# Fifteen extra small loads on ScalarE's DMA queue at the start of a decode kernel

## The chip, the cores and the metric

The kernel runs on one core of one Trainium2 chip. A core has a matrix engine (TensorE, PE in the profile), a vector engine (VectorE, DVE), a scalar engine (ScalarE, ACT), GpSimd (POOL) and SyncE (SP), which here issues the large loads. Sixteen DMA engines move data between HBM and the on-chip memory (SBUF, 128 partitions). The metric is the device time of one execution in microseconds, lower is better: before the change, a median of 381.85 us over three runs (381.73 to 382.11).

## What is computed

One token of a decoder goes through two branches, mixed by a gate:

```python
g = _sigmoid((x * gate_w).sum(-1, keepdims=True))
a = _A_ref(x, A_k_cache, A_v_cache, A_wq, A_wo)
b = _B_ref(x, B_w_in, B_w_sp, B_b_sp, B_w_out)
return g * a + (1 - g) * b
```

Branch A is grouped-query attention for one query position: `x` (1024 values) times `A_wq` (1024 x 4096) gives 32 query heads of 128. They share 4 key/value heads with 65536 cached positions each: scores against `A_k_cache`, softmax, weighted sum of `A_v_cache`, and a product with `A_wo` (4096 x 1024). Branch B is a small gated MLP with one position: `x @ B_w_in` (1024 x 3584), GELU, a layer norm of one half, scaling by `B_w_sp` and a shift by `B_b_sp` (one number each), a product with the other half, and `B_w_out` (1792 x 1024). All tensors are bf16. The two caches are 67 MB each; with the weights some 162 MB are read once.

## The kernel before

**Recording and emission.** The kernel calls `P(engine, function, r=..., w=..., dma=...)` for each operation. A `Recorder` notes which keys an operation reads and writes, works out the waits, and `emit` (from L96) writes each engine's instructions in the recorded order, with semaphore waits in front. A DMA adds 16 to a semaphore of its own name when it has landed. The engines run in order, so a waiting instruction holds up everything behind it on its engine. Two numbers, `R.ahead = 2` and `R.early = 4`, say how many of the first DMAs of SyncE and of ScalarE are moved ahead of the start barrier. At the end SyncE waits for the stores of the output (L122).

**Memory.** One SBUF tensor, the `arena`, holds all regions; a list of names and sizes (from L193) lays them out one behind the other. The first, `RING`, is the landing area of the large loads.

**The large loads.** `load` appends them to a list, and `issue` (L376 to L392) issues the next one on SyncE as soon as the piece of the ring that it overwrites has been used up. The order is A_wq, k(0) with k(1), B_w_in, k(2), k(3), B_w_out, then the remaining keys and values in turn, and A_wo last, whose last quarter is cut into 1280, 512 and 256 KB. Each load has 128 rows, one for each partition, of up to 64 KB. All are issued at L389.

**The small loads.** ScalarE issues four (L288): `x` and `gate_w` as 8 rows of 256 bytes, and the single numbers `B_w_sp` and `B_b_sp`, one row of 2 bytes each. All four stand ahead of the start barrier.

**The start.** `x` is spread over the partitions (L427, L432, L436). At L437 TensorE copies `B_w_sp` and `B_b_sp` to all partitions. DVE forms the gate's products (L442, L443), TensorE sums them (L444), ScalarE takes the exponential (L446, behind the load of its function table), and DVE finishes the gate (L447 to L451). TensorE then multiplies `x` by A_wq (recorded at L260 and L262, as all large matmuls are), and DVE casts and places the queries (L467, L474, L482).

**The body.** For each piece of 16384 positions `k_piece` transposes the keys on DVE in four steps (L502) and multiplies them on TensorE; `score_pair` (L519) takes scores out of PSUM, `exp_pair` (L534) exponentiates on ScalarE, `pt_pair` (L539) transposes, and `pv_piece` multiplies by the values. `mixer_piece`, `mixer_rest` and `wout_piece` do branch B between the first key pieces. The next load into a slot of the ring is issued when its last user, a transpose or a matmul, is done.

**The end.** `wo_rows` and `wo_piece` (L712) multiply by A_wo as its pieces land, DVE casts the result (L775), and SyncE stores 2 KB (L366).

Of the kernel before, what the change touches and what calls it, by code (L numbers as in the profile page):

```python
# [17 lines left out]
class Recorder:  # L18
# [77 lines left out]
    def emit(self, nc):  # L96
        waits = self.plan()
        sems = {e: nc.alloc_semaphore("eng_" + e) for e in self.ENGINES}
        dsem = {k: nc.alloc_semaphore("dma_%s" % k) for k in self.dma_count}
        final = {k: v for k, v in self.dma_count.items()}  # L100

        def run(eng, handle):
            for o, ws in zip(self.ops, waits):
                if o.eng != eng:
                    continue
                for d in ws:
                    if d.dma:
                        handle.wait_ge(dsem[d.dma[0]], d.dma[1])
                    else:
                        handle.wait_ge(sems[d.eng], d.count)  # L110
                last = o.fn(handle)
                if o.dma:
                    last.then_inc(dsem[o.dma[0]], 16)
                elif o.inc:
                    last.then_inc(sems[eng], 1)

        body = nc.cur_bb.bb
        gate = next(i for i, x in enumerate(body.instructions)
                    if isinstance(x, mybir.InstDrain) and x.engine == mybir.EngineType.SP)
        first = len(body.instructions)  # L120
        run("SP", nc.sync)
        nc.sync.wait_ge(dsem["out"], final["out"])  # L122
        made = list(body.instructions)
        moved = made[first:first + self.ahead]
        assert all(isinstance(x, mybir.InstDMACopy) for x in moved)
        body.instructions = made[:gate] + moved + made[gate:first] + made[first + self.ahead:]
        run("POOL", nc.gpsimd)
        run("PE", nc.tensor)
        first = len(body.instructions)
        run("ACT", nc.scalar)  # L130
        made = list(body.instructions)
        gate = next(i for i, x in enumerate(made) if isinstance(x, mybir.InstDrain) and x.engine == mybir.EngineType.Activation)
        moved = made[first:first + self.early]
        assert all(isinstance(x, mybir.InstDMACopy) for x in moved)
        body.instructions = made[:gate] + moved + made[gate:first] + made[first + self.early:]
        run("DVE", nc.vector)


def bass_gated_mix__gqa_block_cached__mixer_gmlp__decode_kernel(
# [23 lines left out]
    FC = FH // 128  # L163
# [12 lines left out]
    QW = DO // NW  # L176
# [11 lines left out]
    def region(name, nbf):  # L188
        nonlocal cur
        OFF[name] = cur  # L190
        cur += (nbf + 15) // 16 * 16

    for name, n in [  # L193
        ("RING", NSUB * SUB), ("KT", NKT * 4096), ("SC", NSC * 2048), ("PSB", 2 * 1024), ("PTSB", 2 * 1024),
        ("QPAD", 4 * QP), ("IDB", 128), ("BM", 256), ("SEL", 16 * 32),
        ("M16", 32), ("MQ", 32), ("XT", KC), ("WB", 2), ("WBB", 4), ("ONEB", 128),
        ("MAXC", 2 * total), ("LP", 2 * total), ("COLS", 2 * 64), ("DM", 64), ("ONES", 256), ("QALL", 128), ("OVZ", 32 * OC + 31), ("E4Z", 128), ("MHALF", 4),
        ("YB", FC), ("OROW", QW),
    ]:
        region(name, n)  # L200
    NA = (cur + 63) // 64 * 64
# [2 lines left out]
    def ab(name, n, o=0):  # L204
        return arena[:, OFF[name] + o:OFF[name] + o + n]
# [4 lines left out]
    def vw(base, off, dims, p0=0, np_=128):  # L210
        ps = base.ap[0][0]
        return bass.AP(tensor=base.tensor, offset=base.offset + off + p0 * ps,
                       ap=[[ps, np_]] + [list(d) for d in dims])
# [41 lines left out]
    P = R.op  # L255
# [42 lines left out]
    small(wb[0:1, 1:2], B_b_sp.rearrange("(a n) -> a n", a=1), "bsp")  # L298

    stream = []
    place = {}
# [41 lines left out]
    for i in range(6):  # L345
        a = 2 * i + 4
# [83 lines left out]
    def f(e):  # L430
        for c in range(KC):
            ins = e.matmul(tb[:, c:c + 1], vw(xm, c, [[8, 128]], 0, 8), oneb[0:8, 0:1], start=(c == 0),  # L432
                           stop=(c == KC - 1), skip_group_check=True)
        return ins
# [374 lines left out]
```

## Time and profile before

| What | Value |
|---|---|
| Median of three runs | 381.85 us (381.73 to 382.11) |
| Span of the profiled execution | 380.3 us |
| The profiled execution's own total time | not given beside its span |
| Mean granted TensorE clock | 0.838 of full speed |
| Bytes read | 162.01 MB, 426 GB/s over the span |
| Busy | TensorE 62%, DVE 54%, ScalarE 6%, GpSimd 2% of the span |

The span runs from the first to the last instruction of the profiled execution. DMA queues have numbers: q1 carries SyncE's DMAs, q10 ScalarE's, q8 instructions fetched while the program runs. A DMA is cut into packets that the sixteen engines work off, and the share of a queue is the time of its packets as a part of sixteen engines' span. In a narrow window a packet counts whole where it starts. An instruction marked ACTq or SPq is the issuing of a DMA, not its transfer. In the timeline each line has the start, the duration, the engine, the line of the kernel and the operands, and in brackets the idle time before it with what ended it. The chain of waits is followed back from the last instruction.

### The profile page before, as it was taken

The numbers are of one execution on the slowest core, as the hardware profiler recorded it, in microseconds if no ns is written. First come the engines' busy times: TensorE is split into PE (matmuls) and PEld (weight loads), VectorE is DVE, ScalarE is ACT, GpSimd is POOL, SyncE is SP. The second block draws the span as 40 slices with busy tenths as digits, with TensorE's granted clock in tenths as the row PEclk, the third lists the DMA queues.
The fourth block names the chain that finished last, engine by engine and source line by source line (L and its number), as shares of the span: only waits on it lengthen the run. The fifth ranks groups of instructions, "written<-read, shape, count | busy, mean of one in ns | idle before, by whom it ended". The sixth has DMA issues, their size and how long they took to land.

```text
span 380.3 us, 2581 instructions
## 1 busy us (share of the span) xinstructions
PE 235.1 (62%) x1449; PEld 58.1 (15%) x836; DVE 204.6 (54%) x162; ACT 23.3 (6%) x24; POOL 8.4 (2%) x37
## 2 busy tenths in 40 slices
PE   0061388458558924895788138952895884739378
PEld 0010011011111200122112001220121110212015
DVE  4011496778389525965892249745774882312020
ACT  1000000010420000002200000022000000220000
POOL 5000000000000000000000000000000000000000
PEclk9998599696859985998699859995899697958689
DMA  9999999999999999999999999999999999999996
GB/s 435 427 420 400 469 388 438 441 469 431 401 414 441 441 443 427 434 410 424 477 441 434 434 434 414 415 441 441 434 407 433 445 441 441 436 403 424 419 426 262
DMA packets 4254, 162.17 MB, mean 426 GB/s; under 512 B 532, under 2 KB 532, under 8 KB 788
## 3 DMA queue, kind: packets, MB, share of 16 engines
q1 hardware_dynamic: 4208, 162.01, 98.9%
q8 instruction: 9, 0.15, 0.2%
q10 hardware_dynamic: 36, 0.00, 0.0%
q14 instruction: 1, 0.01, 0.0%
HBM read 162.01 MB, written 0.00 MB: 426 GB/s over the span
## 4 chain that ended last, share of the span: by engine, by line
DMA 56%; PE 23%; DVE 18%; ACT 1%; issue 1%; SPq 0%; ACTq 0%; DVEq 0%
DMA arena<-in_A_k_cache_dram 34%; DVE arena L502 15%; DMA arena<-in_A_wo_dram 10%; DMA arena<-in_A_v_cache_dram 8%; PE scp L260 7%; PE scp L262 6%; DMA arena<-in_B_b_sp_dram 5%; PE obt L260 4%; PE obt L262 4%; DVE arena L539 1%; PE fbt L712 1%; PE fbt L660 1%; ACT arena L534 1%; SPq L389 0%; ACTq L288 0%
## 5 line engine op out<-in xcount | busy, mean ns | idle before, releaser
L502 DVE STREAM_TRANSPOSE arena<-arena 128x2048 f32<-128x2048 f32 x64 | 143.0, 2284 | 48.2 <-DMA arena<-in_A_k_cache_dram 32.7
L260 PE MATMUL scp<-arena 128*128 128x512 bf16 (+1 forms) x275 | 112.8, 429 | 87.7 <-DVE arena L502 86.3
L262 PE MATMUL scp<-arena 128*128 128x512 bf16 (+1 forms) x279 | 113.1, 427 | 0.0
L260 PE MATMUL obt<-arena 128*64 128x512 bf16 (+2 forms) x334 | 62.9, 419 | 17.5 <-DMA arena<-in_A_v_cache_dram 17.5
L262 PE MATMUL obt<-arena 128*64 128x512 bf16 (+2 forms) x334 | 62.2, 414 | 0.0
L260 PEld LDWEIGHTS scp<-arena 128*128 128x128 bf16 (+1 forms) x275 | 27.7, 104 | 200.1 <-issue 101.3
L539 DVE STREAM_TRANSPOSE arena<-arena 128x2048 bf16<-128x2048 bf16 x7 | 16.2, 2311 | 28.5 <-PE obt L262 26.4
L534 ACT ACTIVATE arena<-arena 128x2048 bf16<-128x2048 f32 x8 | 16.0, 2002 | 218.6 <-DVE arena L531 195.6
L260 PEld LDWEIGHTS obt<-arena 128*64 128x64 bf16 (+1 forms) x334 | 18.3, 113 | 70.7 <-issue 56.1
L519 DVE TENSOR_SCALAR_CACHE_REDUCE arena<-scp 128x2048 f32<-128x2048 f32 x8 | 18.3, 2292 | 16.0 <-PE scp L262 16.0
L580 PE MATMUL mbt<-arena 128*128 128x128 bf16 x16 | 1.9, 258 | 12.6 <-DVE arena L575 12.6
L542 DVE STREAM_TRANSPOSE arena<-arena 128x1024 bf16<-128x1024 bf16 x2 | 2.5, 1246 | 12.7 <-PE obt L262 12.7
L490 POOL COPY arena<-arena 32x32 bf16<-32x32 bf16 x16 | 3.2, 203 | 234.5 <-PE scp L262 209.7
L568 DVE RECIPROCAL arena<-mbt 128x1 f32<-128x1 f32 x4 | 0.6, 139 | 14.1 <-PE mbt L563 14.1
L531 DVE TENSOR_REDUCE arena<-mbt 128x1 f32<-128x32 f32 x4 | 0.8, 192 | 13.5 <-PE mbt L528 13.5
L437 PE MATMUL mbt<-arena 1*128 1x2 bf16 x1 | 0.2, 158 | 12.3 <-DMA arena<-in_B_b_sp_dram 12.3
L439 DVE COPY arena<-mbt 128x2 f32<-128x2 f32 x1 | 0.2, 160 | 12.3 <-PE mbt L437 12.3
L775 DVE CAST arena<-fbt 36x128 bf16<-36x128 f32 x1 | 0.3, 283 | 11.0 <-PE fbt L712 11.0
L432 PE MATMUL scp<-arena 8*128 8x1 bf16 x8 | 0.7, 199 | 8.7 <-DVE arena L427 8.7
L712 PE MATMUL fbt<-arena 128*32 128x128 bf16 x128 | 4.1, 220 | 0.1
L712 PEld LDWEIGHTS fbt<-arena 128*32 128x32 bf16 x128 | 3.6, 97 | 1.6 <-DMA arena<-in_A_wo_dram 0.8
L467 DVE CAST arena<-obt 97x1024 bf16<-97x1024 f32 x1 | 1.2, 1225 | 4.9 <-PE obt L262 4.9
(91 smaller groups left out, 54.2 us busy)
## 6 DMA issues: line engine op xcount, KB each, us to landing
arena<-in_A_k_cache_dram SPq DMA_DIRECT2D x6, 4096.0 KB, 33.1
arena<-in_A_v_cache_dram SPq DMA_DIRECT2D x2, 4096.0 KB, 26.0
arena<-in_B_w_in_dram SPq DMA_DIRECT2D x1, 7168.0 KB, 30.4
arena<-in_A_wo_dram SPq DMA_DIRECT2D x3, 2048.0 KB, 33.4
arena<-in_B_w_out_dram SPq DMA_DIRECT2D x1, 3584.0 KB, 21.5
arena<-in_A_wo_dram SPq DMA_DIRECT2D x1, 1280.0 KB, 30.3
arena<-in_A_wo_dram SPq DMA_DIRECT2D x1, 512.0 KB, 31.0
arena<-in_A_wo_dram SPq DMA_DIRECT2D x1, 256.0 KB, 30.8
```

The source lines that it names most:

```text
L260: return e.matmul(*a, **kw)
L262: one = e.matmul(*a, **kw).ins
L467: P("DVE", lambda e: e.tensor_copy(psb[0:97, :], ob[0:97, :]), w=["psb", "ob"])
L490: P("POOL", lambda e, pb=pb: e.tensor_copy(vw(qpad, 24 + 32 * pb, [[QP, 4], [1, 8]], 32 * pb, 32), vw(qall, 8 * g, [[32, 4], [1, 8]], 32 * ...
L502: P("DVE", lambda e: e.transpose(ktb(i).bitcast(F32), sl[:, 4096 * p:4096 * (p + 1)].bitcast(F32)), r=keys[4 * p:4 * p + 4], w=[("kt", i % ...
L519: P("DVE", lambda e: e.tensor_scalar(scs(j), scp[:, :], 0.0, None, op0=ALU.add, op1=ALU.max, accum_out=maxc[:, j:j + 1]), w=[("sc", j % 2) ...
L534: P("ACT", lambda e: e.activation(psb2, scs(j), ACTF.Exp, bias=gcol(j // 2, K_NB), scale=SCALE, accum_out=lp[:, j:j + 1]), r=[("sc", j % 2 ...
L539: P("DVE", lambda e: e.transpose(ptsb2, psb2), r=["psb"], w=[("ptsb", 0), ("ptsb", 1)])
L542: P("DVE", lambda e: e.transpose(ptsb(n), ab("PSB", 1024, 1024 * (n % 2))), r=["psb"], w=[("ptsb", n % 2)])
L580: ins = e.matmul(mb[:, 0:128], sel[:, 128 * c:128 * (c + 1)], osc[:, 128 * c:128 * (c + 1)], start=(c == 0), stop=(c == 3))
L660: ins = e.matmul(fb[32 * b:32 * (b + 1), 0:QW], e4z[0:97, 31 - j:63 - j], part[0:97, QW * s:QW * (s + 1)], start=(first and s % (NW // 2) ...
L712: ins = e.matmul(fb[32 * b:32 * (b + 1), 0:QW], ovz[:, z:z + 32], sl[:, o:o + QW], start=False, stop=(i == 3 and c == 7), tile_position=(0 ...
```

## The change

A strip `TINY` of 128 bf16 elements per partition is added behind all other regions of the arena. Behind its four small loads ScalarE issues fifteen more: load k (1 to 15) takes k rows of 8 elements (16 bytes) from the first k rows of A_wq, 8192 bytes apart, and writes them to partitions 0 to k-1 of the strip, at columns of its own. Nothing reads the strip. `R.early` stays at 4, so the fifteen stand behind the start barrier and ahead of ScalarE's first table load. All count on one semaphore, `tiny`, and SyncE waits for its full count at the end, behind the wait for the output. The order of all other instructions on every engine is the same as before.

```diff
         nc.sync.wait_ge(dsem["out"], final["out"])
+        nc.sync.wait_ge(dsem["tiny"], final["tiny"])
         made = list(body.instructions)
...
-        ("YB", FC), ("OROW", QW),
+        ("YB", FC), ("OROW", QW), ("TINY", 16 * 8),
     ]:
...
     small(wb[0:1, 1:2], B_b_sp.rearrange("(a n) -> a n", a=1), "bsp")
 
+    for k in range(1, 16):
+        def f(e, k=k):
+            with nc.allow_non_contiguous_dma(reason="a few bytes"):
+                return e.dma_start(ab("TINY", 8, 8 * k)[0:k, :], A_wq[0:k, 8 * k:8 * k + 8])
+        P("ACT", f, w=[("tiny", k)], dma="tiny")
```

## The prediction

> **What bounds the kernel now.** I read the page's totals first, then the windows of ten microseconds, then the chain of waits near the end, then the DMA queues in narrow windows, and last ScalarE's and SyncE's own timelines. The page says:
>
> ```profile
> span 380.3 us, 2581 instructions
> PE 235.1 (62%) x1449; PEld 58.1 (15%) x836; DVE 204.6 (54%) x162; ACT 23.3 (6%) x24; POOL 8.4 (2%) x37
> DMA  9999999999999999999999999999999999999996
> q1 hardware_dynamic: 4208, 162.01, 98.9%
> q8 instruction: 9, 0.15, 0.2%
> q10 hardware_dynamic: 36, 0.00, 0.0%
> ```
>
> No compute engine is busy for more than 62% of the span, while the sixteen DMA engines are busy in every slice but the last. Queue q1 (SyncE's loads) alone takes 98.9% of their time. So the kernel is bound by its loads, and something costs time only if it makes a DMA engine busy longer, leaves the load queue empty, or lengthens the stretch after the last landing. That stretch is in the chain of waits:
>
> ```profile
> 331.05 37.33 DMA arena<-in_A_wo_dram
> ...
> 376.50 1.77 PE fbt L712 x56
> 378.27 0.01 issue
> 378.27 0.42 PE fbt L712 x8
> ...
> 378.79 0.28 DVE arena L775
> ```
>
> and, for what the last eight matmuls wait for, in the timeline of the same stretch:
>
> ```profile
> 378.27 0.23 PEld L712 LDWEIGHTS fbt<-arena 128*32 128x32 bf16 x8 [0.18 <-DMA arena<-in_A_wo_dram]
> ```
>
> The last 256 KB of A_wo release the last eight matmuls at 378.27. Issued at 347.44 and 30.8 us on the way, they land at 378.24. A load counts as landed when the slowest of its DMA engines is done, so the span is the slowest engine's finishing time plus 380.3 - 378.27 = 2.03 us.
>
> The profiled execution's span is 380.3 us. Its own total is not among the figures shown, so I make the sum against the span and carry the difference to the median of the three timed runs, 381.85 us; the 1.55 us between them is taken as fixed. Those three runs spread over 0.38 us (381.73 to 382.11). I call 0.2% (0.76 us) about what a measurement can tell from no change.
>
> **The change, part by part.** Nothing is removed. Four things are added.
>
> *1. Fifteen issues on ScalarE.* They stand behind the start barrier, ahead of the table load for the gate's exponential (L446). ScalarE now does this:
>
> ```profile
> 0.72 0.28 ACTq L288 DMA_DIRECT2D arena<-in_gate_w_dram  x1
> 1.03 0.27 ACTq L288 DMA_DIRECT2D arena<-in_B_w_sp_dram  x1
> 1.34 0.27 ACTq L288 DMA_DIRECT2D arena<-in_B_b_sp_dram  x1
> 2.12 1.28 ACT L446 ACT_TABLE_LOAD   x1 [2.12 <-PEq L794]
> 23.19 0.17 ACT L446 ACTIVATE arena<-scp 128x1 f32<-128x1 f32 x1 [19.78 <-PE scp L444]
> ```
>
> An issue takes 0.27 us whether it covers one row or eight, so 15 x 0.27 = 4.1 us. The table load moves from 2.12 to 6.2 and ends at 7.5. The activation is not wanted before 23.19, when the gate's sum arrives from TensorE: 15.7 us of cover. The longest issue anywhere in the trace is SyncE's 0.94 us (an A_wo load at 330.07); fifteen of those would be 14.1 us, table load done at 17.5, still before 23.19. So this part costs 0 from both ends. If the cover were gone, L446 would hold up DVE's L447 to L451 and behind them, in DVE's order, L467 (the query's cast, at 28.93), with another 4.8 us of slack there.
>
> *2. 120 data packets and their completions on the DMA engines.* The four existing small loads are 8, 8, 1 and 1 rows. If each row goes to an engine of its own with one completion packet behind it, that is 2 x (8+8+1+1) = 36 packets, which is what q10 has. A load of r rows then uses r engines. From the first engine upwards, engine 0 gets all fifteen loads (30 packets), engine 7 eight (16 packets), engine 14 one (2 packets) and engine 15 none: 240 packets in all. How long does one packet hold an engine? I ask for q10's share of sixteen engines in windows that hold few packets. From 4 to 5 us, eight 256-byte data packets:
>
> ```profile
> q10 hardware_dynamic: 8, 0.00, 0.9%
> ```
>
> 0.9% of 16 x 1000 ns over eight is 18 ns each. From 13.84 to 13.87 us, one packet, the two bytes of the w_sp load:
>
> ```profile
> q10 hardware_dynamic: 1, 0.00, 1.9%
> ```
>
> 1.9% of 16 x 30 ns is 9 ns. From 6.5 to 7.1 us, the eight completions of the x load: 0.8% of 16 x 600 ns over eight, again about 9 ns. A 16-byte row stands between the 2-byte and the 256-byte packet and much nearer the first: 9 ns, at most 18. So a new load costs each of its engines 9 + 9 = 18 ns, at most 27. Engine 0 loses 15 x 18 = 0.27 us (at most 0.41), engine 7 0.14, engine 14 0.02, engine 15 nothing; the mean is 240 x 9 / 16 = 0.135 us. What of this reaches the end depends on which engine ends last, and no view that I read names it. The nine 16 KB instruction fetches (q8) load single engines far more unevenly: one, between 55 and 58 us, takes 2.0% of 16 x 3 us = 0.96 us. The slowest engine is therefore likelier one with a fetch or two than engine 0. Ends: 0 (the last engine is 15, or engine 0's loss lies within its lead) and +0.41. I take the mean over engines, +0.14.
>
> Here a rule speaks against the change. The Trainium skill's page "DMA: Bandwidth & Descriptors" says under "Rules for kernel authors" that many small transfers should be made one large one, since below 64 KB one pays mostly overhead, and under "Anatomy of one DMA" gives a fixed cost of about 2.0 us for each (for loads issued from GpSimd). If that cost held a DMA engine, an estimate by the page would be 15 x 2.0 = 30 us on engine 0 and 412 us in all. The q10 rows above say that it is latency, not occupancy, so the sum goes by the rows.
>
> *3. The packets wait their turn, and later ones wait behind them.* The b_sp load is issued at 1.34 and lands 20.2 us later though it is two bytes: engine 0 had eight small packets by then, and 20.2 / 8 = 2.5 us is about one large packet between every two. The fifteen loads stand behind b_sp on the same queue, so x, gate_w, w_sp and b_sp keep their landings, and so does L437, which waits for b_sp. The last new load lands near 21.5 + 30 x 2.5 = 97 us. Nobody reads the strip, which lies behind all other regions of the arena, so no address moves. Cost 0.
>
> *4. One more wait on SyncE, behind the wait for the output.* It is met since about 97 us, so it costs one instruction at the very end: between 0 and 0.04 us (the gap between neighbouring instructions in the chain, "368.38 0.04 issue"). Nothing is queued behind it. I take 0.04.
>
> Sum: 0 + 0.14 + 0 + 0.04 = +0.18 us, bounds 0 and +0.45. Span 380.5, time 381.85 + 0.18 = 382.0 us.
>
> **Rivals.**
>
> *A. ScalarE's queue is too short for nineteen loads, and the issues block (slower).* The trace shows only four in flight on q10. For it: a blocked ScalarE keeps the gate's exponential, and DVE behind it, waiting. Against: on SyncE's queue nine were in flight near 347.5 us (two v loads of 26 us to landing, six A_wo loads, a store) and the ninth was issued in 0.35 us. Price: with room for N, the nineteenth is issued when number 19 - N has landed. With N = 9 that is the sixth new one, at 21.5 + 6 x 5.0 = 51.5 us; with issue and table load L446 runs near 53. DVE then needs 0.9 us (L447 to L451), 2.8 us (28.93 to 31.69: L467 to L482) and 10.6 us (41.32 to 51.91: the four transposes of k(0)) before SyncE can issue k(3), near 67.5. The queue runs dry after 8.4 + 8.4 + 7.3 + 4.2 = 28.3 MB at 426 GB/s, also near 67.5. So nine is where it begins to decide, and each place fewer costs two packets, 5 us: N = 8 gives 387 us, N = 4 some 407.
>
> *B. The rows are not spread (slower).* The trace shows the spreading only for 8 rows and 1 row. If loads of other row counts all ran on engine 0, it would get 120 data packets and 15 completions, 135 x 9 = 1.2 us, and would be the slowest engine: 381.85 + 1.2 + 0.04 = 383.1 us. It decides from 0.76 / 0.009 = 85 packets on one engine. Against it: 8 is no more special than 15 as far as the 36 packets tell. The Trainium skill's page "DMA: Bandwidth & Descriptors", section "Why a DMA increments its semaphore by 16 and not by 1", has the rule: the largest number up to 16 that divides the slowest dimension of both sides, on the lowest engines. By it r rows use r engines, as in the forecast; no row here shows it for 3, 7 or 15. A dearer 16-byte packet on the spread engines acts alike, from 25 ns each (30 x 25 ns = 0.75 us).
>
> *C. Staggering helps (faster).* The engines get a staircase of delays, and large packets that start apart might collide less. But the busy share leaves 1.1% of 380.3 = 4.2 us; the start (no bytes in the first half microsecond, 131 GB/s in the second) takes 1.0 of it and the stretch after the last landing 2.0. At most 1.2 us are to be had: 380.7 us. Against: a staircase of 18 ns steps is small beside packets of 2.5 us.
>
> *D. The loads do not run as written:* had they no effect at all, the time would be 381.85, inside the forecast.
>
> **How the numbers follow.** Forecast, with D: 0.66, own range 381.6 to 382.4 (0 to +0.45, widened by the runs' spread). B with dearer packets: 0.15. A: 0.08. C: 0.06, of which half passes 0.76 us. Something slower that I don't see: 0.05. The range 381.3 to 383.2 holds the forecast, B and the weaker half of C, 0.84; A and the unseen are left out. Slower: nearly all of A, B and the unseen, 0.27. Faster: 0.04. Within 0.2%: 0.69.
>
> **What would show it.** Right: q10 has 36 + 240 = 276 packets and still about 0.0%; the table load of L446 begins near 6.2 and its ACTIVATE stays near 23.2; k(3) is still issued near 52; the last A_wo piece lands within 0.4 us of 378.24. B: q10 has 36 + 135 = 171 packets. A: an issue of microseconds on ScalarE, and L446 far behind 23.2. C: the last landing more than 0.7 us earlier. I would be wrong above all if a small packet delays the large one behind it by more than its own 9 ns, which the shares can't show, or if the slowest engine changes.

## The result and the profile after

The changed kernel takes 382.94 us (median of six runs, 382.4 to 383.5) against 381.89 us (six runs, 381.73 to 382.11): a ratio of 1.003, with a 95% interval from 1.002 to 1.0039. It is slower by about 1.05 us. That is small, but clear of the noise, and its runs spread over 1.1 us where those of before spread over 0.38.

The profiled execution took 383.05 us with a span of 381.7 us. From its page:

```profile
span 381.7 us, 2594 instructions
DMA  9989999999999999999999999999999999999995
q1 hardware_dynamic: 4208, 162.01, 98.7%
q8 instruction: 9, 0.15, 0.2%
q10 hardware_dynamic: 276, 0.01, 0.0%
```

Queue q10 has 276 packets, so load k does use k engines (36 + 240), and the new packets still take no visible share. The DMA engines remain the bound. The 8 in the third slice of the span, 19 to 29 us, is no idle time: a packet counts whole in the slice where it starts, and 50 packets of 64 KB start there against 61 before, the others just past its end. ScalarE's timeline is as forecast in its order:

```profile
2.13 5.29 ACTq L306 DMA_DIRECT2D arena<-in_A_wq_dram  x15
7.46 1.28 ACT L453 ACT_TABLE_LOAD   x1 [7.46 <-issue]
23.25 0.17 ACT L453 ACTIVATE arena<-scp 128x1 f32<-128x1 f32 x1 [14.51 <-PE scp L451]
```

The fifteen issues take 5.3 us instead of 4.1, and still 14.5 us are to spare before the exponential (L453 here, L446 before), which runs at 23.25 as against 23.19.

Where the time came from is seen in the chain of waits, from the points at which it passes through a landing. Of the kernel before (start, duration, what):

```profile
29.30 39.76 DMA arena<-in_A_k_cache_dram
117.37 28.07 DMA arena<-in_A_k_cache_dram
331.05 37.33 DMA arena<-in_A_wo_dram
```

And of the changed kernel:

```profile
28.67 41.07 DMA arena<-in_A_k_cache_dram
118.83 27.85 DMA arena<-in_A_k_cache_dram
332.28 37.51 DMA arena<-in_A_wo_dram
...
379.69 0.42 PE fbt L719 x8
```

Adding start and duration, the landings move from 69.06 to 69.74 (+0.7 us), from 145.44 to 146.68 (+1.2), from 368.38 to 369.79 (+1.4), and the last eight matmuls from 378.27 to 379.69 (+1.4). So the load stream falls behind early and doesn't catch up.

How it falls behind is seen in the DMA queues of a window that holds one large packet per engine, from 25.3 to 27.7 us. The columns are packets, MB, share of sixteen engines in the window. Before:

```profile
q1 hardware_dynamic: 16, 1.05, 100.8%
```

After:

```profile
q1 hardware_dynamic: 16, 1.05, 107.3%
q10 hardware_dynamic: 12, 0.00, 0.3%
```

Sixteen packets of 64 KB took 100.8% of 2.4 us each before, that is 2.42 us, and 107.3%, 2.575 us, after. The twelve small packets themselves take 0.3%, some 10 ns each. **The small packets are cheap; it is the large packets behind them that take longer**, on average 0.16 us in this window. In the window from 18.3 to 20.7 us, while the stream still reads A_wq, the changed kernel shows nothing of it:

```profile
q1 hardware_dynamic: 16, 1.05, 100.8%
q10 hardware_dynamic: 14, 0.00, 0.3%
```

For the rest of this document I sum this up from the packet records of each trace: the *excess* is the time that large packets took beyond the undisturbed duration of their size (2.418 us for 64 KB, 2.116 for 56 KB, 1.215 for 32 KB), over all engines, from 20.5 to 70 us. It is 0.7 us before and 13.3 us after. Behind a 16-byte packet a large one is held up by 0.114 us in the mean of 87 cases, at most by 0.30. Spread over sixteen engines, 13.3 - 0.7 = 12.6 us are 0.8 us each, which is most of the 1.05 us measured. Four fifths of it (87 x 0.114 = 9.9 us) lie on packets directly behind a 16-byte one, the rest on other large packets. The engines don't lose alike, and a load has landed when the slowest is done: between the two profiled executions, the first of an A_wo load's sixteen landings moves by 0.5 us and the last by 1.3. Of this 1.3, some 0.5 appears only between 88 and 107 us, after the last small packet (72 us): an 8 KB instruction fetch (queue q14) and the packet behind it take one engine 0.95 us longer at 87.2 us, and that engine is then the last to land, at 107.5; in the kernel before, the engine with the same fetch at 85.6 us does not become the last. So what one execution loses depends also on which engine such a fetch meets.

### The profile page after: what moved, and what is told of

Its sections match the earlier page's. It is cut to its first block, busy times and chain, and to the rows that moved or that the text cites. A ratio compares the mean times of both kernels' runs of the same rounds, so it can differ in the third digit from the quotient of the medians.

```text
span 381.7 us, 2594 instructions
## 1 busy us (share of the span) xinstructions
PE 231.5 (61%) x1447; PEld 57.9 (15%) x836; DVE 204.3 (54%) x162; ACT 23.3 (6%) x24; POOL 9.4 (2%) x37
## 4 chain that ended last, share of the span: by engine, by line
DMA 57%; PE 22%; DVE 19%; ACT 1%; issue 1%; ACTq 0%; SPq 0%; DVEq 0%
DMA arena<-in_A_k_cache_dram 34%; DVE arena L509 16%; DMA arena<-in_A_wo_dram 10%; DMA arena<-in_A_v_cache_dram 8%; PE scp L261 5%; PE scp L263 5%; DMA arena<-in_B_b_sp_dram 5%; PE obt L261 4%; PE obt L263 4%; DVE arena L546 1%; PE fbt L719 1%; PE fbt L667 1%; ACT arena L541 1%; ACTq L289 0%; SPq L396 0%
## 5 line engine op out<-in xcount | busy, mean ns | idle before, releaser
L261 PE MATMUL scp<-arena 128*128 128x512 bf16 (+1 forms) x273 | 110.3, 421 | 88.6 <-DVE arena L509 87.5
L263 PE MATMUL scp<-arena 128*128 128x512 bf16 (+1 forms) x279 | 111.6, 419 | 0.5 <-issue 0.5
L261 PE MATMUL obt<-arena 128*64 128x512 bf16 (+2 forms) x334 | 62.1, 412 | 21.3 <-DMA arena<-in_A_v_cache_dram 21.3
L263 PE MATMUL obt<-arena 128*64 128x512 bf16 (+2 forms) x334 | 61.3, 406 | 0.0
L526 DVE TENSOR_SCALAR_CACHE_REDUCE arena<-scp 128x2048 f32<-128x2048 f32 x8 | 18.3, 2292 | 16.0 <-PE scp L263 16.0
L446 DVE COPY arena<-mbt 128x2 f32<-128x2 f32 x1 | 0.2, 159 | 12.7 <-PE mbt L444 12.7
```

The costliest lines, as they stand in the source:

```text
L261: return e.matmul(*a, **kw)
L263: one = e.matmul(*a, **kw).ins
L526: P("DVE", lambda e: e.tensor_scalar(scs(j), scp[:, :], 0.0, None, op0=ALU.add, op1=ALU.max, accum_out=maxc[:, j:j + 1]), w=[("sc", j % 2) ...
```

## The experiments

All kernels below have the fifteen loads on ScalarE and the wait at the end; they differ in what the loads read, or in where they are issued. Each was timed against the kernel before on the same chip. Nothing reads the strip, so the output is the full one in all of them. The time is the median of all runs of a kernel, the excess that of its one profiled execution, whose own time can lie elsewhere in the spread: 381.94 us for keys_4096, 383.2 for all_eight, 382.56 for late.

| Run | Rows of the loads | Distance of rows | Time, us | Ratio (95%) | Excess, us |
|---|---|---|---|---|---|
| before | none | | 381.89 | | 0.7 |
| changed | 1 to 15, A_wq | 8192 B | 382.94 | 1.003 (1.002 to 1.0039) | 13.3 |
| one_row | 1, A_wq | one row only | 381.78 | 1.0 (0.9991 to 1.0008) | 0.7 |
| all_fifteen | 15, A_wq | 8192 B | 383.25 | 1.0035 (1.0021 to 1.0049) | 13.5 |
| src_gate | 1 to 15, gate_w | 128 B | 381.9 | 1.0002 (0.9993 to 1.0011) | 1.4 |
| src_keys | 1 to 15, keys | 8192 B | 383.25 | 1.0035 (1.0022 to 1.0047) | 14.9 |
| wq_near | 1 to 15, A_wq | 128 B | 382.0 | 1.0003 (0.9994 to 1.0012) | 2.0 |
| keys_8448 | 1 to 15, keys | 8448 B | 381.93 | 1.0005 (0.9996 to 1.0014) | 0.5 |
| one_far | 1, row k-1 of A_wq | 8192 B from load to load | 381.83 | 1.0 (0.9991 to 1.0009) | 1.2 |
| late | 1 to 15, A_wq, issued at 108 us | 8192 B | 382.27 | 1.0012 (1.0003 to 1.0021) | 0.8, and 6.8 from 110 to 150 us |
| keys_4096 | 1 to 15, keys | 4096 B | 382.32 | 1.0014 (1.0005 to 1.0023) | 3.5 |
| keys_2048 | 1 to 15, keys | 2048 B | 381.93 | 1.0003 (0.9994 to 1.0012) | 0.7 |
| all_four | 4, A_wq | 8192 B | 381.89 | 1.0001 (0.9992 to 1.001) | 1.1 |
| all_eight | 8, A_wq | 8192 B | 382.65 | 1.0029 (1.0018 to 1.0039) | 10.3 |

The first four runs ask what it is about the loads that costs. Theory P: a price that each small read has. Theory C: several engines reading small rows at the same moment. Theory S: where the rows are read from. Beside them stands the staircase itself, which sets the engines apart.

**One row in each load.**

```diff
-                return e.dma_start(ab("TINY", 8, 8 * k)[0:k, :], A_wq[0:k, 8 * k:8 * k + 8])
+                return e.dma_start(ab("TINY", 8, 8 * k)[0:1, :], A_wq[0:1, 8 * k:8 * k + 8])
```

> Fifteen loads of one row each, so all fifteen data packets should fall on one DMA engine and no other engine has any. Theory P (price): a 16-byte read holds up the large packet behind it, wherever it stands, by about 0.11 us in the mean of the changed kernel's trace once the A_wq load is over. Then one engine alone loses about 12 x 0.11 = 1.3 us, the last landing of each later load moves by about that, the first landing by nothing, and the time is near 383.0. Theory C (collision): the delay comes from several engines reading small rows at the same moment. One engine alone then loses next to nothing and the time is 381.9 to 382.1.

Measured: 381.78 us, no change. Fifteen reads after 20.5 us held up the packets behind them by 0.000 us in the mean. On one engine alone a small read costs nothing; theory P falls for that case. The fifteen issues and the wait at the end cost nothing that can be measured either.

**Fifteen rows in each load.**

```diff
-                return e.dma_start(ab("TINY", 8, 8 * k)[0:k, :], A_wq[0:k, 8 * k:8 * k + 8])
+                return e.dma_start(ab("TINY", 8, 8 * k)[0:15, :], A_wq[0:15, 8 * k:8 * k + 8])
```

> Fifteen loads of fifteen rows each: 225 data packets instead of 120, fifteen on each of fifteen engines, no staircase. Theory P: the engine that had the most has no more than before, so the time stays near 383, but the first fifteen landings are now all late: excess summed over the engines rises from 13 us to some 24 us. Theory C: fifteen engines read at once in every step, so each read costs more than 0.11 us; the time goes to 384 or above. If the staircase itself was the cause (engines set apart), the time falls back to 382.0.

Measured: 383.25 us, excess 13.5 us. The staircase is not the cause, since there is none here and the kernel is as slow. Both other expectations missed in part. The sum did not rise to 24 us as P wanted, and the price of one read did not rise as C wanted: it fell to 0.056 us over 189 reads, because from 50 us on it costs nothing here (0.3 us of excess from 50 to 70 us, beside 2.4 us in the changed kernel), which I can't explain. Nor did the run give theory C what it supposes: fifteen reads at once came seldom, as at 21.0 and 41.3 us; mostly the trace has seven and eight in turn, a large packet apart.

**The rows from gate_w.**

```diff
-                return e.dma_start(ab("TINY", 8, 8 * k)[0:k, :], A_wq[0:k, 8 * k:8 * k + 8])
+                return e.dma_start(ab("TINY", 8, 8 * k)[0:k, :], gate_w.rearrange("(i n) -> i n", n=64)[0:k, 0:8])
```

> As the change, but the rows are read from gate_w (2 KB in all, rows 128 bytes apart) instead of from A_wq (rows 8192 bytes apart). Theory S (source): the delay comes from where the small rows lie in HBM against what the large stream reads at that moment; rows of 8192 bytes pitch in another tensor are its bad case, and with gate_w the excess of the large packets between 20 and 70 us falls from 13 us to under 3 us and the time to 382.0. Theories P and C: no change from the changed kernel, 382.9.

Measured: 381.9 us and 1.4 us of excess, as theory S said. The number of packets, the engines, the destinations, the issues and the wait are those of the change. In the window from 25.3 to 27.7 us this run shows eleven small packets, and large ones that are not held up:

```profile
q1 hardware_dynamic: 16, 1.05, 100.8%
q10 hardware_dynamic: 11, 0.00, 0.3%
```

So all of the loss hangs on where the small rows are read from.

**The rows from the keys.**

```diff
-                return e.dma_start(ab("TINY", 8, 8 * k)[0:k, :], A_wq[0:k, 8 * k:8 * k + 8])
+                return e.dma_start(ab("TINY", 8, 8 * k)[0:k, :], A_k_cache[0, 0].rearrange("(p x) d -> p (x d)", x=32)[0:k, 8 * k:8 * k + 8])
```

> As the change, but the rows are read from the keys that the second large load reads, again 8192 bytes apart. Theory S, in the form that a small read costs something only when the stream beside it reads another tensor: now the reads during the A_wq load (9 to 20.5 us) are held up, up to 0.25 us each, which they were not, and those during the key load (20.5 to 41 us) are free, which they were not. Theories P and C: as the changed kernel, 382.9, nothing before 20.5 us and some 13 us of excess after it.

Measured: 383.25 us and 14.9 us of excess, again next to none during the A_wq load (0.2 us from 4 to 20.5 us). The form of theory S that I had written, another tensor than the stream's, is refuted: reading the very keys that the stream reads is as dear as reading A_wq.

What src_gate and the dear runs still differ in is the distance between the rows (theory D) and the tensor (theory T). The next runs part these, and try one engine alone and another place in the kernel.

**A_wq with 128 bytes between rows.**

```diff
-                return e.dma_start(ab("TINY", 8, 8 * k)[0:k, :], A_wq[0:k, 8 * k:8 * k + 8])
+                return e.dma_start(ab("TINY", 8, 8 * k)[0:k, :], A_wq[0].rearrange("(i n) -> i n", n=64)[0:k, 0:8])
```

> As the change, from A_wq too, but the rows are 128 bytes apart in its first row instead of 8192. Theory D (distance): the cost comes from several engines reading small rows a power of two of some thousand bytes apart at the same moment; with 128 bytes there is none: excess of large packets between 20 and 70 us under 3 us in sum, 381.9. Theory T (tensor): a small read is dear where it comes out of a large tensor, and gate_w was cheap for its place; then the excess stays near 13 us and the time at 382.9 to 383.3.

Measured: 382.0 us, excess 2.0 us. The tensor is not the cause.

**The keys with 8448 bytes between rows.**

```diff
-                return e.dma_start(ab("TINY", 8, 8 * k)[0:k, :], A_wq[0:k, 8 * k:8 * k + 8])
+                return e.dma_start(ab("TINY", 8, 8 * k)[0:k, :], A_k_cache[0, 0, 0:495].rearrange("(p x) d -> p (x d)", x=33)[0:k, 8 * k:8 * k + 8])
```

> As the run that read the small rows from the keys (383.25, 15 us of excess), but 8448 bytes apart, 256 more than 8192. Theory D in its narrow form (rows 8192 bytes apart fall on the same part of HBM): the 256 bytes break it, excess under 5 us, 381.9 to 382.2. In its wide form (any rows that far apart): as before, 383.2. Theory T: 383.2.

Measured: 381.93 us and 0.5 us of excess, against 383.25 and 14.9 with 256 bytes less between the rows. This is the sharpest of the runs. The same window once more, of the run with 8192 bytes:

```profile
q1 hardware_dynamic: 16, 1.05, 105.5%
q10 hardware_dynamic: 12, 0.00, 0.3%
```

and of the run with 8448:

```profile
q1 hardware_dynamic: 16, 1.05, 100.8%
q10 hardware_dynamic: 12, 0.00, 0.3%
```

Twelve small packets among sixteen large ones in both: the large ones are held up only where the small rows are 8192 bytes apart. Two of the eleven runs with 8448 bytes took longer than any run of before, 382.36 and 382.77 us; the profile is of another, of 381.84, and can't say why.

**One row in each load, each from another row of A_wq.**

```diff
-                return e.dma_start(ab("TINY", 8, 8 * k)[0:k, :], A_wq[0:k, 8 * k:8 * k + 8])
+                return e.dma_start(ab("TINY", 8, 8 * k)[0:1, :], A_wq[k - 1:k, 8 * k:8 * k + 8])
```

> Fifteen loads of one row, load k reading row k-1 of A_wq, so successive reads are 8192 bytes apart but one engine makes them all, one about every 5 us. Theory C (collision of engines) with D: no cost, 381.8 to 382.0, no excess behind a small packet. If a far small read is dear by itself: 12 reads at 0.11 to 0.13 us on one engine, last landings 1.3 to 1.6 us later and the time 383.2.

Measured: 381.83 us, 0.000 us behind a small packet in the mean (at most 0.006). Reads 8192 bytes apart made by one engine, one after the other, cost nothing, so it takes loads that use several engines. That their reads must fall on the same moment does not follow, and the changed kernel's own trace speaks against it. Its read at 23.82 us has no other small read within 2 us, and the packet behind it takes 0.24 us longer; this is the window around it, with that one read and eleven completions, where before has 100.8%:

```profile
q1 hardware_dynamic: 16, 1.05, 101.7%
q10 hardware_dynamic: 12, 0.00, 0.3%
```

In all, some fifteen of its reads have at most four others within 0.6 us, and they hold up a packet by about 0.09 us in the mean, against some 0.12 us for the others. In the runs with one row such lone reads cost nothing. So a delay depends on more than the small reads of that moment, perhaps on how earlier delays have shifted the engines against each other; that stays open.

**The loads issued later.**

```diff
         exp_pair(i + 1)
+        if i == 0:
+            tiny()
         pv_piece(2 * i + 1)
```

(`tiny()` is the loop of the change, taken from its place.)

> The same fifteen loads from A_wq, 8192 bytes apart, but issued behind the second exponential of the attention (about 109 us), where the load stream brings values and keys. Theory: whatever makes the packets of the A_wq load immune is a matter of that load, not of the place in the kernel, so packets of 64 KB of keys and values are held up as those of the first key load were: excess of some 10 to 15 us in sum between 109 and 185 us, and 382.7 to 383.4. If the cost belongs to the start of the kernel (the engines still in step with each other), there is none here and the time is 381.9.

Measured: 382.27 us, +0.36 us and barely clear of zero, and 6.8 us of excess from 110 to 150 us, where before has 1.4. The packets of keys and values are held up too, so it is not a matter of the kernel's start alone; but it costs about a third of what the change costs, between the two expectations. By then the engines are further apart: the packet records of before have the sixteen landings of one load within 0.5 us at 21 us and within 1.8 us at 126 us, so fewer small reads fall together. That this is why the loss is smaller is not shown, and the records don't bear it out: reads of this run with no other within 0.6 us hold up a packet by some 0.04 us in the mean (without one beside an instruction fetch), those in groups of six or more by about as much.

The last four runs ask how the loss depends on the distance and on the number of engines.

**4096 and 2048 bytes.**

```diff
-                return e.dma_start(ab("TINY", 8, 8 * k)[0:k, :], A_wq[0:k, 8 * k:8 * k + 8])
+                return e.dma_start(ab("TINY", 8, 8 * k)[0:k, :], A_k_cache[0, 0].rearrange("(p x) d -> p (x d)", x=16)[0:k, 8 * k:8 * k + 8])
```

and with `x=8` for 2048 bytes.

> As the run from the keys with 8192 bytes between the small rows, now with 4096. With 8192 the time was 383.25 and the excess 15 us, with 8448 it was 381.93 and none. If rows collide because a step of 8192 returns to the same part of HBM, a step of 4096 returns to it with every second row: half the rows meet, 2 to 8 us of excess, 382.1 to 382.7. If only 8192 and above collide: none, 381.9. If any power of two of some thousand bytes is alike: 15 us, 383.2.

> The same with 2048 bytes: if the step must return to the same part, every fourth row meets, excess of 0 to 4 us and 381.9 to 382.3; if all powers of two are alike, 15 us and 383.2.

Measured: 382.32 us with 3.5 us of excess at 4096 bytes; 381.93 us with 0.7 us, the value of before, at 2048. The profile at 4096 bytes is of a run of 381.94 us, near the lowest of eleven (381.91 to 382.91), so 3.5 us understate what the median run loses. The loss falls off as it should if a distance of 8192 bytes brings every row back to the same part of HBM, 4096 every second and 2048 every fourth; that part itself is seen in no trace. The second and third readings (only 8192 and above; all powers of two alike) are excluded.

**Four and eight rows in each load.**

```diff
-                return e.dma_start(ab("TINY", 8, 8 * k)[0:k, :], A_wq[0:k, 8 * k:8 * k + 8])
+                return e.dma_start(ab("TINY", 8, 8 * k)[0:4, :], A_wq[0:4, 8 * k:8 * k + 8])
```

and with `[0:8]` on both sides for eight.

> Fifteen loads of four rows each from A_wq, 8192 bytes apart: 60 data packets on four engines, fifteen each. Collision of small reads alone: a read that meets three others costs less than one that meets fourteen, 0 to 0.05 us in the mean, last landings less than 0.6 us later, 381.9 to 382.4. If the number did not matter as long as it is more than one: 12 reads x 0.11 us = 1.3 us on these four engines, 383.

> The same with eight rows on eight engines, 120 data packets as in the change, but fifteen on each of eight engines. Collision: between the run with four and that with fifteen rows (383.25): 382.2 to 383.0, excess of 3 to 8 us between 20 and 70 us. If only the total of small packets counted: 382.9.

Measured: 381.89 us with four engines, 0.005 us behind a small packet; 382.65 us with eight, ratio 1.0029, 0.077 us behind a small packet and 10.3 us of excess, more than the 3 to 8 us that I had put down. The seven runs with eight engines fall in two groups, 382.43 to 382.65 and 383.2 to 383.72, and the profile is of the second. So loads on four engines are free, and loads on eight are not. But eight reads at once are not dear by themselves. The window in which the change has 107.3% holds eight of them in this run, all for nothing:

```profile
q1 hardware_dynamic: 16, 1.05, 100.8%
q10 hardware_dynamic: 8, 0.00, 0.2%
```

The eight reads at 21.0, 25.9, 30.7 and 35.6 us lengthen the sixteen large packets beside them by 0.00, 0.00, 0.06 and 0.18 us in sum; those at 40.6 and 42.9 us by 1.6 and 1.2. In all_fifteen seven reads at 23.6 and eight at 26.0 us, after fifteen at 21.0, cost 1.1 and 2.0 us. So the number of the moment does not decide alone, and why the loss begins where it does is not shown. Nor do these runs part the number of engines from the number of packets: all_four has only 60 data packets, on the lowest four engines, against 120.

## Why the prediction missed its likeliest case

The time of 382.94 us lies inside the range (381.3 to 383.2), but the case I called likeliest, no measurable change at 382.0 us (0.69), did not come; slower by more than 0.2%, which I gave 0.27, did. The measured time lies outside the forecast's own 381.6 to 382.4. That the wide range holds it is owed to rival B, and in part to luck: the 383.1 that set the upper end was the price of packets piled on one engine, which did not happen.

- **Part 1, the issues: right that they cost nothing.** They took 5.3 us instead of 4.1, all of it covered; the run with gate_w as the source has the same issues and is unchanged.
- **Part 2, the packets: this is the step that failed.** I put a packet at "9 ns, at most 18" and took the mean over engines, +0.14 us. The duration was right: the 276 packets still take 0.0% of the engines' time. But I took a packet's own duration for all that it does to its engine. The large packet behind it took 0.114 us longer in the mean, over twelve times the 9 ns: in place of +0.14 us, the changed kernel's packets cost 12.6 / 16 = 0.8 us in the mean over engines, and the latest landings moved by 1.3 to 1.4 us, where I had called 0.4 us the limit. I had named this as the first way to be wrong, and had given a dearer packet a chance of 0.15, but no term in the sum. My rows for the price, the x, gate_w and w_sp loads, could not show this: they all ran beside the A_wq load, where small packets cost next to nothing in any run, and their rows lie 256 bytes apart or alone. So I had bounded the unknown from rows that shared conditions under which it is zero. That the slowest engine would likelier be one with an instruction fetch than engine 0 held: at 107.5 us it is one.
- **Part 3, the order: right.** b_sp releases TensorE at 21.73, before at 21.67. The waiting itself cost nothing, as I wrote; the last small packet starts at 72 us rather than 97, because packets of later loads are shorter.
- **Part 4, the wait at the end: not contradicted.** The run with gate_w, which has the same wait, is 0.04 us above before, but that lies within its interval around zero.
- **Rival A (blocked issues): excluded.** The nineteen loads were issued without a pause, in 5.3 us for the last fifteen.
- **Rival B: half right.** The rows are spread, as 276 packets show. The Trainium skill's page "DMA: Bandwidth & Descriptors", section "Why a DMA increments its semaphore by 16 and not by 1", said that r rows go to r engines, and the count agrees for all of 1 to 15. But the variant that I put in one sentence, a dearer small read from 25 ns on, is nearest to what happened; only that the price was neither the packet's own nor the same for every source.
- **Rival C (staggering helps): no sign of it.** The run with equal numbers on fifteen engines is slower too, 383.25 us.

## What to carry to other kernels

The price of a small DMA is not its packet's duration: look at the large packets that run behind it, by the share and the count of packets in a window of one packet's length, and take the row from a stretch in which the same stream runs. Where small loads use eight or more DMA engines beside a saturated load stream, choose rows that are not 4 or 8 KB apart; 256 bytes more between them took the loss in the median from 1.4 us to nothing. Small loads on one or four engines, or with rows 2 KB and less apart, were free here or nearly so.

## What the hardware showed that I had not expected

- Small reads 8192 bytes apart, from loads that use eight to fifteen engines, can hold up the large packet behind each, in the changed kernel by 0.11 us in the mean and up to 0.3; at 8448, 2048 and 128 bytes there is next to nothing, at 4096 less (0.43 us of time against 1.39). The dependence on the distance is shown. That rows 8192 bytes apart share a part of HBM, where the reads queue, is the likeliest reading, and argued; by itself it does not say why eight reads at once cost nothing at 26 us in one run and 2 us in another.
- The Trainium skill's page "DMA: Bandwidth & Descriptors", section "Latency and other measured facts", tells of a loss that depends on the row distance too, for large copies between HBM tensors: 207 GB/s with rows 512 KB apart, 164 at 2 MB, 103 at 4 MB, where a pad of 192 bytes did not help and one of 4 KB did. Here 16-byte rows at 8 KB show a loss, and a pad of 256 bytes was enough. No run here had rows as far apart as that table's, and none shows that the cause is the same.
- While the stream reads A_wq, up to 20.5 us, small reads cost next to nothing in any run, from whichever tensor they come (the excess from 4 to 20.5 us is 0.31 us in sum at most). That need not be a matter of the A_wq load. In the kernels with rows 8192 bytes apart at most ten reads fall together there, and the first step of thirteen or fifteen, at 20.9 us, is the first that costs; in all_eight the loss begins only at about 40 us, near the end of the first key load. What sets the beginning stays open; a run with fifteen reads at once during the A_wq load would tell more.
